# Twelve operand tiles laid out first in SBUF, each beginning at a multiple of 2048 bytes

## The chip, the cores and the metric

The kernel runs on one core of a Trainium2 chip. The metric is the device time of one launch in microseconds (us). [...]

## The reference

Linear attention over 8 batches of 8 heads, 576 positions and 64 channels per head; its 4608 x 512 result runs through two feed-forward networks with a squared ReLU.

```python
q_s = softmax of q over channels;  k_s = softmax of k over positions
kv = einsum('bhsd,bhse->bhde', k_s, v);  attn = einsum('bhsd,bhde->bhse', q_s, kv)
x = attn.transpose(0, 2, 1, 3).reshape(4608, 512)
x = relu(x @ w_in)**2 @ w_out          # 512 -> 2048 -> 512
x = relu(x @ w2_in)**2 @ w2_out        # 512 -> 2048 -> 512
```

## The kernel before

Tokens go in nine blocks (j) of 512, the hidden width in 16 chunks (f) of 128, or 8 pairs (a), or 4 units (u). Every fp32 operand of a large product is split into a high and a low part, and `passes` (line 400) issues three matmuls for a term: low x high, high x low, high x high. A matmul on PE is two instructions: LDWEIGHTS loads the stationary operand (128 columns), MATMUL streams the moving one (256 or 512 columns) through it. PE goes through four stages:

- **h** (`h_mm`, 1728 matmuls of 512 columns): attention, block by block, and the first product of network 1, x against `w0`. Small matmuls of the attention (`kvps`, `xps`) lie between.
- **y0** (`second_mm`, l=0, 3024 matmuls of 256 columns): the second product of network 1. The moving operand is G (the hidden values), the stationary one W. A profile row calls it `y<-G,W`.
- **m** (`first_mm`, 3024 of 256): the first product of network 2, moving x, stationary W (`m<-x,W`).
- **y1** (`second_mm`, l=1, 3024 of 256): the second product of network 2. Here W moves and G is stationary (`y<-W,G`).

The last three use a seven-product scheme for 2 x 2 blocks (`LEFT`, `RIGHT`, `ORDER`, lines 36 to 38): `comb_add`, `comb_hi` and `comb_lo` (lines 76 to 97) make seven combinations, each with a high and a low part, of every operand. One call of `second` for one a is 7 results x 2 halves x 3 passes = 42 matmuls; a block j has 8 of them, 336 matmuls.

Operands live in twelve slots of 14,336 bytes per partition, `w0` to `w7` and `hl0` to `hl3`. A combination in a slot is 1024 bytes, a high part lies 7168 bytes from its low one, and a stationary operand is 512 bytes, so a moving operand begins at a multiple of 1024 bytes from its slot's start and a stationary one at a multiple of 512. W of pair a lies in `w{(a+5)%8}` (`slot_of`, line 706); G of block j, pair a in `hl{(8j+a+1)%3}`, but for the last four of a network (line 923); x of network 2 in two of the four `hl`. In stage h, chunk f of `w0` lies in slot `w{f//3}`, f = 15 in `hl3`, and x in `hl0` for an even j, `hl1` for an odd one, its last quarter in `hl3`. There too moving operands begin at multiples of 2048 and stationary ones at multiples of 512 from the slot's start.

`schedule` (line 542) sets the order of all instructions from planned costs and due times, once, when the kernel is built. It knows tags of slots, and no addresses. The tile pool gives each tag its place in SBUF when a tile of that tag is first asked for, one behind the other. This gives the slots these first bytes:

| slot | first byte | mod 512 | slot | first byte | mod 512 |
|---|---|---|---|---|---|
| w0 | 116416 | 192 | w6 | 52448 | 224 |
| w1 | 155392 | 256 | w7 | 66784 | 224 |
| w2 | 175936 | 320 | hl0 | 100032 | 192 |
| w3 | 9344 | 128 | hl1 | 190272 | 320 |
| w4 | 23680 | 128 | hl2 | 213824 | 320 |
| w5 | 38112 | 224 | hl3 | 136896 | 192 |

Of the kernel before, what the change touches and what calls it, by code (L numbers as in the profile page):

```python
# [8 lines left out]
F32 = mybir.dt.float32  # L9
# [11 lines left out]
P = 128  # L21
NP = H // 2
TB = 512
HB = TB // 2
# [17 lines left out]
def linear_attention_two_relu2_ffn(ctx: ExitStack, tc: tile.TileContext, q0, k0, eye, qh, kh, vh, wio, out):  # L42
# [10 lines left out]
    pool = ctx.enter_context(tc.tile_pool(name="sb", bufs=1))  # L53
    psum = ctx.enter_context(tc.tile_pool(name="ps", bufs=1, space=bass.MemoryType.PSUM))
    dram = ctx.enter_context(tc.tile_pool(name="dr", bufs=1, space=bass.MemoryType.DRAM))

    def f32(ap):
        return ap.bitcast(F32)
# [994 lines left out]
```

## Time and profile before

| | |
|---|---|
| median of 3 runs | 1610.34 us (1607.62 to 1617.39) |
| the profiled execution's own time | 1607.12 us |
| its span, first to last instruction | 1605.0 us |
| PE, busy | 1556.1 us (97%), 11,664 matmuls |
| PEld (LDWEIGHTS), busy | 1457.0 us (91%) |
| DVE, ACT, POOL busy | 74%, 59%, 25% |
| granted PE clock, mean | 0.991 |

Busy time of PE counts a matmul from its start to the modelled end of its pipeline, so that matmuls overlap in it: the mean duration of one says little, and the distance between the starts of two neighbours says what it costs. Where PE never stops, that distance is the length of a stretch divided by the matmuls that begin in it. Matmuls that still run at a stretch's edge are counted in it too.

### The profile page before, as it was taken

The page shows a single profiled execution, that of the slowest core. Times are in us where ns is not written, and L with a number is a line of the kernel's source. Part 1 is how long each engine was busy: PE and PEld are TensorE (multiplying, and loading weights), DVE is VectorE, ACT ScalarE, POOL GpSimd, SP SyncE. Part 2 cuts the span into 40 slices and gives each one's busy share as a digit, 9 for nine tenths or more (in the row PEclk, how much of TensorE's full clock was granted, in tenths as well). Part 3 has the DMA queues.
Part 4 walks back from the last instruction along what each step waited for, and adds up shares of the span by engine and source line. Part 5 has one row for each costly group of instructions (what it writes and reads, how often), then busy time and mean ns, then how long its engine had stood idle before and what let it go on. Part 6 is the DMA issues. An engine that isn't in the chain of part 4 may idle for free. (4 is left out here: it accounts for less than half of the span.)

```text
span 1605.0 us, 29964 instructions
## 1 busy us (share of the span) xinstructions
PE 1556.1 (97%) x11664; PEld 1457.0 (91%) x11664; DVE 1194.9 (74%) x1755; ACT 953.1 (59%) x1605; POOL 400.8 (25%) x332
## 2 busy tenths in 40 slices
PE   6799999999999999999998999999999899999998
PEld 4578888878888999999998999999999899999997
DVE  7998887777544988888889954553347898898885
ACT  7766766566554655555556877776667444333332
POOL 1000000000023333332323433333221443333322
PEclk9999999999999999999999999999999999999999
DMA  8547776676664443444434576663346344344332
GB/s 327 168 129 230 249 227 226 217 233 217 210 195 159 145 132 132 133 134 134 135 107 154 171 220 213 213 216 135 135 135 191 111 149 132 131 143 134 132 106 79
DMA packets 139135, 270.49 MB, mean 169 GB/s; under 512 B 12145, under 2 KB 71665, under 8 KB 138993
## 3 DMA queue, kind: packets, MB, share of 16 engines
q1 hardware_dynamic: 138992, 268.58, 51.2%
q8 instruction: 91, 1.49, 0.4%
q14 instruction: 52, 0.42, 0.1%
HBM read 161.58 MB, written 106.95 MB: 167 GB/s over the span
## 5 line engine op out<-in xcount | busy, mean ns | idle before, releaser
L404 PE MATMUL h<-hl,w 128*128 128x512 f32 x1620 | 395.7, 399 | 10.6 <-DVE w L64 10.6
L404 PEld LDWEIGHTS h<-hl,w 128*128 128x128 f32 x1620 | 303.7, 190 | 80.2 <-DVE w L64 10.0
L404 PE MATMUL m<-x,W 128*128 128x256 f32 x3024 | 362.2, 282 | 8.2 <-DVE W L97 5.3
L404 PEld LDWEIGHTS m<-x,W 128*128 128x128 f32 x3024 | 359.9, 189 | 9.8 <-DVE W L97 5.9
L404 PE MATMUL y<-W,G 128*128 128x256 f32 x3024 | 357.7, 280 | 7.8 <-DVE G L97 7.7
L404 PEld LDWEIGHTS y<-W,G 128*128 128x128 f32 x3024 | 356.3, 189 | 8.6 <-DVE G L97 8.4
L404 PEld LDWEIGHTS y<-G,W 128*128 128x128 f32 x3024 | 358.3, 189 | 0.7 <-DVE G L97 0.5
L404 PE MATMUL y<-G,W 128*128 128x256 f32 x3024 | 358.7, 281 | 0.3 <-DVE G L97 0.3
L92 ACT ACTIVATE G<-hl 128x512 fp32r<-128x512 f32 (+1 forms) x108 | 94.5, 889 | 163.7 <-PE y L404 101.7
L97 DVE TENSOR_TENSOR G<-hl,G 128x512 fp32r<-128x512 f32 (+1 forms) x108 | 121.5, 1126 | 34.3 <-ACT G L92 34.3
L434 POOL TENSOR_TENSOR ts<-ts,ts 128x512 f32<-128x512 f32 x54 | 85.0, 1574 | 245.2 <-ACT ts L431 218.7
L391 ACT ACTIVATE r<-h 128x512 f32<-128x512 f32 x144 | 84.9, 591 | 65.4 <-PE h L404 54.7
L443 DVE TENSOR_TENSOR t<-m,ts 128x512 f32<-128x512 f32 x72 | 49.7, 691 | 94.8 <-PE m L404 89.3
L258 POOL PARTITION_ALL_REDUCE m<-m x28 | 24.4, 872 | 337.5 <-DVE m L254 112.7
L449 ACT ACTIVATE t<-t 128x512 f32<-128x512 f32 x144 | 90.1, 629 | 2.8
L97 DVE TENSOR_TENSOR G<-att,G 128x1280 fp32r<-128x1280 f32 x50 | 75.8, 1516 | 10.4 <-ACT G L92 10.4
L97 DVE TENSOR_TENSOR G<-cf,G 128x1280 fp32r<-128x1280 f32 x50 | 77.3, 1546 | 8.4 <-ACT G L92 8.0
L92 ACT ACTIVATE G<-qd 128x512 fp32r<-128x512 f32 x40 | 25.3, 632 | 87.2 <-PE y L404 45.8
L92 ACT ACTIVATE G<-att 128x1280 fp32r<-128x1280 f32 x50 | 63.1, 1263 | 13.3 <-DVE att L84 13.3
L92 ACT ACTIVATE G<-cf 128x1280 fp32r<-128x1280 f32 x50 | 63.2, 1264 | 12.0 <-DVE cf L84 11.0
L446 ACT ACTIVATE t<-t 128x512 f32<-128x512 f32 x72 | 45.3, 629 | 38.9 <-DVE t L443 37.6
L92 ACT ACTIVATE G<-qc 128x512 fp32r<-128x512 f32 x40 | 25.3, 631 | 67.0 <-PE y L404 45.0
(162 smaller groups left out, 1991.0 us busy)
## 6 DMA issues: line engine op xcount, KB each, us to landing
g<-r SPq DMA_DIRECT2D x144, 256.0 KB, 3.5
g<-t SPq DMA_DIRECT2D x144, 256.0 KB, 2.8
hl<-g SPq DMA_DIRECT2D x64, 512.0 KB, 3.8
raw<-wio SPq DMA_DIRECT2D x48, 512.0 KB, 4.8
qc<-g SPq DMA_DIRECT2D x40, 512.0 KB, 3.8
qd<-g SPq DMA_DIRECT2D x40, 512.0 KB, 3.8
y<-t SPq DMA_DIRECT2D x72, 256.0 KB, 2.3
w<-wf SPq DMA_DIRECT2D x48, 256.0 KB, 4.8
```

Of the source, the lines that this page charges most:

```text
L92: nc.scalar.activation(out=hls[key][:, 0, r], in_=src, func=AF.Copy)
L97: nc.vector.tensor_tensor(out=hl[:, 1, r], in0=src, in1=f32(hl[:, 0, r]), op=ALU.subtract)
L258: nc.gpsimd.partition_all_reduce(m[:, 1, :P], m[:, 0, :P], P, bass.bass_isa.ReduceOp.max)
L391: nc.scalar.activation(out=r0[j, f].rearrange("p a b -> p (a b)"), in_=m.pop(("h", j, f)), func=AF.Relu)
L404: nc.tensor.matmul(ps, a, b, start=start, stop=True, skip_group_check=True)
L434: nc.gpsimd.tensor_tensor(out=t[k, "s5"], in0=t[k, "s5"], in1=t[k, "s2"], op=ALU.add)
L443: nc.vector.tensor_tensor(out=temp(k, q), in0=m[k, i], in1=t[k, "s5"], op=ALU.add)
L446: nc.scalar.activation(out=t[k, q], in_=t[k, q], func=AF.Relu)
L449: nc.scalar.activation(out=t[k, q], in_=t[k, q], func=AF.Square)
```

## The change

Right after the pools are opened, one tile of 896 bytes per partition and then one tile for each of the twelve slots are asked for. None of them is written or read. As a tag gets its place when it is first asked for, the twelve slots come first: from byte 2048 on (1152 bytes are taken by the DMA scratch and constants), 14,336 = 7 x 2048 bytes each, in the order w0 to w7, hl0 to hl3, and all others come behind them. Each slot's first byte is 0 mod 2048. The other tiles move too: the attention's operands (`kvbd`, `qd`) to multiples of 1024, the temporaries, sources and raw weights to other multiples of 32.

```diff
     dram = ctx.enter_context(tc.tile_pool(name="dr", bufs=1, space=bass.MemoryType.DRAM))
+
+
+    pool.tile([P, 224], F32, name="margin", tag="margin")
+    for tag in [f"w{i}" for i in range(8)] + [f"hl{i}" for i in range(4)]:
+        pool.tile([P, 14 * HB], F32, name=f"{tag}_room", tag=tag)
 
     def f32(ap):
```

All instructions of the five engines, their order, their waits and their shapes stay as they are; the addresses of their operands are all that differs.

## Rows read from the trace of the kernel before

**Rows 1.** Page, part 1: busy us (share of the span) xinstructions.
```profile
PE 1556.1 (97%) x11664; PEld 1457.0 (91%) x11664; DVE 1194.9 (74%) x1755; ACT 953.1 (59%) x1605; POOL 400.8 (25%) x332
```

**Rows 2.** Busy time by stage: stretch, length, busy (count) by engine, clock, DMA, GB/s.
```profile
100.00:504.53 404.53, 404.36 (x2178) 327.30 (x2177) 282.18 (x616) 249.23 (x584) 38.12 (x41) 1.00 0.66 214
504.53:863.38 358.85, 358.54 (x3025) 358.20 (x3024) 306.06 (x338) 208.69 (x236) 109.45 (x93) 1.00 0.41 134
863.38:1215.64 352.26, 344.11 (x2883) 342.48 (x2881) 191.77 (x244) 259.85 (x423) 117.80 (x82) 1.00 0.56 179
1215.64:1605.00 389.36, 373.74 (x3170) 372.75 (x3168) 327.08 (x360) 160.58 (x192) 123.81 (x98) 0.99 0.40 130
```

**Rows 3.** Page, part 5: PE's large groups, count, busy, mean ns, idle before.
```profile
L404 PE MATMUL h<-hl,w 128*128 128x512 f32 x1620 | 395.7, 399 | 10.6 <-DVE w L64 10.6
...
L404 PE MATMUL m<-x,W 128*128 128x256 f32 x3024 | 362.2, 282 | 8.2 <-DVE W L97 5.3
...
L404 PE MATMUL y<-W,G 128*128 128x256 f32 x3024 | 357.7, 280 | 7.8 <-DVE G L97 7.7
...
L404 PE MATMUL y<-G,W 128*128 128x256 f32 x3024 | 358.7, 281 | 0.3 <-DVE G L97 0.3
```

**Rows 4.** PE in whole blocks: y0, j 1-7; m, 2-7; y1, 2-7; h, 8.
```profile
545.02:823.41 278.39, 278.39 (x2355) 1.00 0.40 129
953.15:1191.52 238.37, 238.37 (x2018) 1.00 0.55 176
1321.50:1557.54 236.04, 236.04 (x2019) 1.00 0.39 130
460.36:504.53 44.17, 44.17 (x193) 1.00 0.51 169
```

**Rows 5.** PE in stage y0, block j=2, pairs a=3 to 7, one row each.
```profile
599.81:604.79 4.98, 4.98 (x44) 1.00 0.53 178
604.79:609.56 4.77, 4.77 (x44) 1.00 0.35 120
609.56:614.59 5.03, 5.03 (x45) 1.00 0.32 104
614.59:619.54 4.95, 4.95 (x45) 1.00 0.34 108
619.54:624.49 4.95, 4.95 (x45) 1.00 0.32 105
```

**Rows 6.** PE, one pair each: y0 j=4 a=3, j=5 a=4; y1 j=1 a=5, j=4 a=4.
```profile
679.36:684.39 5.03, 5.03 (x44) 1.00 0.34 116
...
724.11:728.87 4.76, 4.76 (x44) 1.00 0.33 110
...
1306.94:1311.96 5.02, 5.02 (x44) 1.00 0.23 79
...
1420.13:1424.90 4.77, 4.77 (x44) 1.00 0.60 204
```

**Rows 7.** PE in stage h: j=8 f=0-2, j=8 f=3-5, j=7 f=1-2, j=7 f=10-11.
```profile
460.36:468.53 8.17, 8.17 (x38) 1.00 0.67 221
468.53:476.93 8.40, 8.40 (x38) 1.00 0.48 149
...
416.69:422.26 5.57, 5.57 (x25) 1.00 0.83 244
442.98:448.54 5.56, 5.56 (x26) 1.00 0.67 229
```

**Rows 8.** Waits of PE: total us, times, longest us; the two longest.
```profile
PE h L404 <- DVE w L64: 10.6, 8, 2.7
PE y L404 <- DVE G L97: 8.0, 3, 6.9
```

**Rows 9.** VectorE at line 97, two sources: ns minimum/median/maximum, first and last start.
```profile
L97 DVE TENSOR_TENSOR G<-att,G x50: 1475/1485/2210, 462.0 to 1589.2; 128x1280 fp32r<-128x1280 f32 x50
L97 DVE TENSOR_TENSOR G<-cf,G x50: 1474/1486/2201, 464.2 to 1584.2; 128x1280 fp32r<-128x1280 f32 x50
```

## The prediction

> **What bounds the kernel now.** I began with the page's first part: PE is busy for 97% of the span, no other engine for more than 74% [rows 1]. The busy time by stage then shows where it ever stops. Through the 404.53 us of stage h that follow the first 100 it is busy for 404.36, through the 358.85 of y0 for 358.54 [rows 2]; the large groups had to wait 10.6, 8.2, 7.8 and 0.3 us in all, beside 1474 us of busy time [rows 3], and the longest sums of waits are for VectorE's operands at a stage's start [rows 8]. So the time is PE's own pace: the distance between the starts of two neighbouring matmuls, times their number. PEld, which loads the next matmul's stationary operand, is busy for 358.20 of y0's 358.85 us [rows 2]: two streams out of SBUF run side by side all the time, the moving operand and the next stationary one.
>
> The next thing to see is that this pace is not one number. [...] Within one block of y0 five neighbouring pairs of 42 matmuls take 4.98, 4.77, 5.03, 4.95 and 4.95 us [rows 5]. The length of a pair repeats for the same two slots in other blocks [rows 5, 6].
>
> What orders these lengths is where the two operands lie. I call **offset** the first byte of the moving operand's slot less that of the stationary one's, mod 512; inside a slot both operands begin at multiples of 512, so every matmul of a pair has the same one. With G's and W's slots from the table of places, the five pairs have the offsets 128 (hl2, w0), 448 (hl0, w1), 0 (hl1, w2), 192 (hl2, w3) and 64 (hl0, w4). The two slowest numbers of the table recur at offset 0: 5.03 us again for hl0 over w0, and 5.02 in y1, where w2 moves over hl2. The quickest recur at 448: 4.76 for hl0 over w1, 4.77 in y1 for w1 over hl1 [rows 6]. Offset 0 is thus seen with slots at 192 and at 320 mod 512, and with either operand in either role; 448 with a moving slot at 192 and at 256. Shifting both operands together changed nothing, shifting one against the other changed 5%. The slots that this compares lie at many distances, so the rest of the address seems to matter little.
>
> For 512 columns the order is another one. In stage h 36 matmuls at offset 0 take 8.17 us, 226.9 ns each, and 36 at offset 448 take 8.40, 233.3 ns; offsets 128 and 192 (block 7: 24 matmuls in 5.57 and in 5.56) cost 232.1 and 231.7 [rows 7]. There offset 0 is the best.
>
> **The change part by part.** No instruction is added, removed or moved on any queue; the extra tiles are neither written nor read. What changes is that all twelve slots begin at 0 mod 512, so **every large matmul gets offset 0**.
>
> The 256-column stages: I price one matmul at 5.03 / 42 = 119.8 ns, the rows of offset 0. y0: 3024 x (119.8 - 118.4) = +4.4 us. m: 3024 x (119.8 - 118.2) = +4.7. y1, the quickest now: 3024 x (119.8 - 117.1) = +8.2. Together +17.3 us, all on the path, as PE's starts are the path. The least certain is m, whose operands change slots every six matmuls, so that no stretch of it shows an offset by itself; without it the sum would be +12.6.
>
> Stage h: even blocks cost 230.1 ns [rows 4], odd ones 232.1 and 231.7 where rows show them [rows 7], 230.9 over five even and four odd. Offset 0 gives 226.9, 4.0 less. Block 0 lies in the first 100 us, where PE waits 10.6 us for operands [rows 8] and would only wait longer; 8 x 192 = 1536 matmuls are left, 6.1 us at most. Small matmuls of the attention cut into seven of these eight blocks, and the row of 226.9 is from the undisturbed one, so I take three quarters: -4.6 us. This gain needs suppliers that keep up with a PE under 2% quicker: in that stage VectorE is busy for 282 of 404.53 us, ScalarE for 249, DMA for 0.66 of its time [rows 2], so they do.
>
> Not priced: the attention's own matmuls, some 640 of the 2178 in stage h. Their places change too and no row separates them; at the 6.2 ns between the ends of [rows 5] they are 4.0 us either way, and I take nothing. VectorE, ScalarE and POOL write and read at new places; the same VectorE instruction has medians of 1485 and 1486 ns from its two sources `att` and `cf`, which lie apart and write to all `hl` slots [rows 9], so I take nothing there either, and if some got longer, PE's slower pace in m, y0 and y1 gives them room.
>
> Sum: +17.3 - 4.6 = **+12.7 us**. Against the profiled execution's own 1607.12 us (span 1605.0) that is 1619.8; against the median of the runs shown, 3.2 us above that execution, 1623.0. I forecast 1622. The forecast's own range is 1615 (m gains nothing) to 1628 (nothing comes back in h).
>
> **The rivals.**
>
> *Places do not matter* (0.10). The lengths of the pairs would then come from what else runs beside them, such as VectorE's and POOL's accesses, and stay. Time 1607 to 1610. Against it: the same length returns for the same slots in other blocks and in y1, beside other work [rows 5, 6]. [...]
>
> *Straddling, and so faster* (0.15). All slow pairs at offset 0 have both operands at an odd multiple of 64 bytes, where a read might cross lines that an even place does not; the quick ones have one at an even multiple (w1 at 256). No row has both at an even one, which is what the change makes. If that were the cause, all 256-column matmuls would go at 4.77 / 42 = 113.6 ns: 3024 x (4.8 + 4.6 + 3.5) = -39.0, with -4.6 in h -43.6 us: about 1565. Against it: in stage h both operands at an odd multiple is the best case, not the worst [rows 7]; and a pair with w3 at 128 or w4 at 128, even multiples as well, took 4.95, not 4.77 [rows 5].
>
> *Slower by more, no gift in h* (0.13). Offset 0 was seen in h only with x in hl0 and w0. If two streams at the same multiple of 2048 disturb each other at 512 columns as they do at 256, stage h goes to the worst it shows, 233.3 ns instead of 230.9: 1536 x 2.4 = +3.7 in place of -4.6. Then +21.0: 1628 by the profiled execution, 1631 by the median, over 1% slower. The point from which it decides: a block of 192 matmuls over 44.4 us.
>
> That the change does not do what it says is ruled out by the places themselves: the twelve first bytes are 2048 + 14336 i.
>
> **How the numbers follow.** The forecast has 0.62. About 1% (16 us) is what a measurement of this kernel can tell from no change; my +12.7 lies just inside it, and with what h may fail to give back and some us between medians about a quarter of it, 0.16, lies outside. Slower by over 1%: 0.16 + 0.13 = 0.29. Within 1%: 0.46 + 0.10 = 0.56. Faster by over 1%: 0.15. The range goes from 1606 (nothing changes) to 1633 (the third rival on the median, with 2 us for the runs' scatter) and leaves out the second rival and a tail.
>
> **What would show it.** In the changed kernel's profile a block of 336 matmuls in y0, m and y1 should take 40.2 us each, where now it is 39.8, 39.7 and 39.3; a pair 5.03 us everywhere, with no 4.77 left; stage h's last block 43.6 us for 44.17; VectorE's medians at 1485 ns. PE's waits in the large groups should stay near 27 us. Pairs that keep their old mixture speak for the first rival, pairs at 4.77 for the second. The forecast is wrong as well if offset 0 with both slots at an even place has a length of its own that no row shows.

## The result, and the profile after

The changed kernel takes **1623.58 us** in the median (1617.73 to 1628.77, 7 runs) where the kernel before, run beside it, takes 1610.69 (1607.62 to 1617.39, 7 runs): a ratio of 1.0069, 95% interval [1.0048, 1.0091]. It is slower by 0.7%, clear of noise and within 1%. The forecast was 1622, its range 1606 to 1633. The profiled execution has a span of 1620.1 us (before 1605.0) and a time of its own of 1622.16 (before 1607.12).

The busy time of each stage, with the columns of [rows 2], for stage h after its first 100 us, y0, m and y1:

```profile
100.00:504.19 404.19, 400.82 (x2180) 327.18 (x2179) 282.63 (x617) 249.19 (x585) 38.72 (x41) 1.00 0.66 215
504.19:867.06 362.87, 362.87 (x3026) 362.87 (x3024) 305.98 (x339) 209.09 (x236) 110.23 (x93) 1.00 0.39 132
867.06:1222.53 355.47, 348.91 (x2882) 347.49 (x2881) 190.96 (x243) 259.63 (x423) 117.34 (x82) 1.00 0.54 178
1222.53:1620.10 397.57, 382.77 (x3170) 382.11 (x3168) 327.55 (x360) 160.32 (x192) 118.78 (x98) 0.99 0.37 127
```

Against [rows 2] the stages are longer by -0.34, +4.02, +3.21 and +8.21 us, 15.1 in all, which is the whole difference of the two spans. In the last three it is PE's busy time that grew, by 4.33, 4.80 and 9.03 us; the time in which PE stood still there shrank from 24.1 to 21.4 (6.56 in m and 14.80 in y1). In stage h it is the other way: PE is busy for 3.5 us less and stands still for 3.37 us where it was 0.17.

Whole blocks, as in [rows 4] (length of the stretch, PE's busy time and count, granted clock as a share of full speed, DMA):

```profile
544.50:826.74 282.24, 282.24 (x2355) 1.00 0.38 128
955.61:1198.05 242.44, 242.22 (x2018) 1.00 0.53 174
1329.84:1571.76 241.92, 241.92 (x2019) 1.00 0.37 127
460.67:504.19 43.52, 43.52 (x194) 1.00 0.52 174
```

The three 256-column stages now run at one pace: 282.24 / 2352 = 120.0 ns, 242.44 / 2016 = 120.3 (with 0.22 us of stops in it), 241.92 / 2016 = 120.0. In block j=2 of y0 pairs a=3 and 4, and in stage h the first 36 matmuls of the last block:

```profile
599.94:604.98 5.04, 5.04 (x45) 1.00 0.54 176
604.98:610.02 5.04, 5.04 (x45) 1.00 0.30 107
460.67:468.83 8.16, 8.16 (x38) 1.00 0.61 194
```

The mixture of [rows 5] is gone: pair a=3 took 4.98, a=4 took 4.77, and both take 5.04 now. Stage h's 36 matmuls take 8.16 us, as only w0's did [rows 7], and its whole last block goes at 43.52 / 192 = 226.7 ns, whatever the slot. VectorE's two instructions at [rows 9] keep their medians to 1 ns:

```profile
L102 DVE TENSOR_TENSOR G<-att,G x50: 1473/1486/2198, 463.2 to 1604.1; 128x1280 fp32r<-128x1280 f32 x50
L102 DVE TENSOR_TENSOR G<-cf,G x50: 1474/1485/2204, 465.4 to 1599.6; 128x1280 fp32r<-128x1280 f32 x50
```

And this is what PE waited for in stage h from 100 us on (total us, times, longest):

```profile
PE xps L372 <- DVE qhl L69: 2.1, 3, 1.4
PE h L409 <- ACT hl L66: 0.7, 1, 0.7
PE h L409 <- DVE hl L69: 0.6, 2, 0.4
```

That is 3.4 us. The kernel before has one wait in that stretch, 0.2 us for `qhl`.

### The profile page after: what moved, and what is told of

It is laid out like the page before. It is cut to its first block, busy times and chain, and to the rows that moved or that the text cites. A ratio compares the mean times of both kernels' runs of the same rounds, so it can differ in the third digit from the quotient of the medians.

```text
span 1620.1 us, 29964 instructions
## 1 busy us (share of the span) xinstructions
PE 1570.7 (97%) x11664; PEld 1475.9 (91%) x11664; DVE 1194.9 (74%) x1755; ACT 953.1 (59%) x1605; POOL 396.7 (24%) x332
## 5 line engine op out<-in xcount | busy, mean ns | idle before, releaser
L409 PE MATMUL m<-x,W 128*128 128x256 f32 x3024 | 367.3, 284 | 6.6 <-DVE W L102 5.4
L409 PE MATMUL y<-W,G 128*128 128x256 f32 x3024 | 366.5, 284 | 6.9 <-DVE G L102 6.9
L409 PEld LDWEIGHTS m<-x,W 128*128 128x128 f32 x3024 | 365.3, 193 | 8.0 <-DVE W L102 6.0
L409 PEld LDWEIGHTS y<-W,G 128*128 128x128 f32 x3024 | 365.4, 193 | 7.4 <-DVE G L102 7.3
L409 PEld LDWEIGHTS y<-G,W 128*128 128x128 f32 x3024 | 363.0, 192 | 0.1
L409 PE MATMUL y<-G,W 128*128 128x256 f32 x3024 | 363.0, 283 | 0.0
```

The costliest lines, as they stand in the source:

```text
L409: nc.tensor.matmul(ps, a, b, start=start, stop=True, skip_group_check=True)
```

## The experiments

All are edits of the changed kernel, and in all of them the instructions and their order stay the same. "Offset" is, as in the prediction, the first byte of the moving operand's slot less that of the stationary one's, mod 512. The experiments ran in three groups, each beside the kernel before; its median there was 1615.59, 1612.86 and 1611.31 us, so times are compared within a group and by ratios. Each trace is of one execution, and the start of a launch varies: the 2178th matmul before the first of y0 begins between 99.7 and 104.6 us in the eleven kernels' traces, at a granted clock of 0.88 to 0.93 over the first 100 us. Where the length of stage h matters, it is therefore given from this matmul on too.

The theory: the offset sets PE's pace. The rival: each operand's own place sets it, and what is slow is an even place.

### Everything 64 bytes further: all64

```diff
-    pool.tile([P, 224], F32, name="margin", tag="margin")
+    pool.tile([P, 112], F32, name="margin", tag="margin")
```

> All twelve slots begin at 64 mod 512 (and not at multiples of 2048), so the offset between moving and stationary operand stays 0. Theory (the offset between the two operands sets PE's pace): as the changed kernel, 120 ns for every 256-column matmul, 40.3 us per block of 336, span 1620 within 3 us. Rival (each operand's own place sets it, an even place is the slow one): both operands leave it, pace back to 118 or below, span 1605 or less.

Measured: ratio 1.008 [1.0063, 1.0096], as slow as the changed kernel. Whole blocks of y0, m and y1:

```profile
549.67:831.90 282.23, 282.23 (x2354) 1.00 0.38 128
960.45:1202.57 242.12, 242.12 (x2018) 1.00 0.55 174
1334.40:1576.32 241.92, 241.92 (x2018) 1.00 0.38 127
```

The lengths are those of the changed kernel to 0.32 us, with every slot at an odd multiple of 64 bytes and no longer at one of 2048. The rival that even places are slow falls. The span, 1624.6, lies a little over the 1623 that was expected: 4.5 us over the changed kernel's, of which 3.6 arise before the 2178th matmul, where the first 100 us have a granted clock of 0.90 here and of 0.93 there.

### One operand 64 bytes from the other: w64 and hl64

```diff
-    pool.tile([P, 224], F32, name="margin", tag="margin")
-    for tag in [f"w{i}" for i in range(8)] + [f"hl{i}" for i in range(4)]:
+    pool.tile([P, 96], F32, name="margin", tag="margin")
+    for tag in [f"hl{i}" for i in range(4)]:             # hl64: the eight w first
+        pool.tile([P, 14 * HB], F32, name=f"{tag}_room", tag=tag)
+    pool.tile([P, 16], F32, name="pad", tag="pad")
+    for tag in [f"w{i}" for i in range(8)]:              # hl64: the four hl behind them
         pool.tile([P, 14 * HB], F32, name=f"{tag}_room", tag=tag)
```

> hl slots at 0 mod 512, w slots at 64: offset 448 in y0, m and h, 64 in y1. Theory: y0 and m go at 113.4 ns (38.1 us per block of 336), y1 at 113.4 or 117.8 ns (38.1 to 39.6 us), stage h at 233.3 ns (last block of 192: 44.8 us). Against the changed kernel -40 us in y0 and m, -7 to -20 in y1, +8 in h: span 1568 to 1582. Rival (each operand's own place): one of two operands leaves the even place, so less than all64 gains: span between 1605 and 1620.

> w slots at 0 mod 512, hl slots at 64: offset 64 in y0, m and h, 448 in y1. Theory: y1 at 113.4 ns (38.1 us per block of 336), y0 and m at 113.4 or 117.8 ns (38.1 to 39.6 us), h at 229 ns (last block of 192: 44.0 us): -20 us in y1, -13 to -40 in y0 and m, +2 in h, span 1560 to 1588. Rival (each operand's own place): as w64, between 1605 and 1620.

Measured: w64 ratio 0.9901 [0.9881, 0.9921], profiled span 1594.3; hl64 ratio 0.9876 [0.9832, 0.992], profiled span 1599.8, and one of its four runs at 1586.95 us where the others lie at 1599.56 to 1601.88. Whole blocks of y0, m and y1 and stage h's last block, w64:

```profile
547.22:813.78 266.56, 266.56 (x2355) 1.00 0.41 136
942.47:1179.90 237.43, 237.43 (x2018) 1.00 0.55 177
1309.23:1546.67 237.44, 237.44 (x2018) 1.00 0.39 129
462.80:507.55 44.75, 44.75 (x194) 1.00 0.50 168
```

and hl64:

```profile
552.77:829.79 277.02, 277.02 (x2355) 1.00 0.40 130
959.81:1197.25 237.44, 237.44 (x2018) 1.00 0.56 177
1325.15:1553.63 228.48, 228.48 (x2018) 1.00 0.40 134
```

Sixty-four bytes between the two kinds of slot are worth some 2% of the kernel against all64 (0.9901 and 0.9876 over 1.008). Where the offset is 448 (y0 of w64, y1 of hl64) a matmul costs 266.56 / 2352 = 228.48 / 2016 = 113.3 ns; where it is 64 (y1 of w64, y0 of hl64) 237.44 / 2016 = 277.02 / 2352 = 117.8. Swapping which slots were shifted swapped the quick stage from y0 to y1, as the operands' roles swap there. The rival, by which both spans would lie between 1605 and 1620, falls. But the theory as it stood missed both spans too (1568 to 1582 and 1560 to 1588). In w64 the miss is m, which has offset 448 and runs at 237.43 / 2016 = 117.8 ns, not 113.4: at an offset of 448 the run shows two paces. In hl64 most of it is stage h, which ends 8.8 us later than in the changed kernel where 2 was expected; 3.8 of them arise before the 2178th matmul.

### All offsets in one run: sweep64 and sweep32

```diff
-    pool.tile([P, 224], F32, name="margin", tag="margin")
-    for tag in [f"w{i}" for i in range(8)] + [f"hl{i}" for i in range(4)]:
+    pool.tile([P, 96], F32, name="margin", tag="margin")
+    for tag in [f"hl{i}" for i in range(4)]:
         pool.tile([P, 14 * HB], F32, name=f"{tag}_room", tag=tag)
+    for i in range(8):
+        if i:
+            pool.tile([P, 16], F32, name=f"pad{i}", tag=f"pad{i}")    # sweep32: 8
+        pool.tile([P, 14 * HB], F32, name=f"w{i}_room", tag=f"w{i}")
```

> hl slots at 0 mod 512, slot w0 at 0, w1 at 64, and so on to w7 at 448: one run shows eight offsets in y0 (0, 448, 384, ... 64 for w0 to w7) and the eight negative ones in y1 and, for w0 to w4, in h. Theory: in y0 a pair of 42 takes 5.04 us with W in w0 and 4.77 with W in w1; 4.95 to 4.99 at offsets 64, 128, 192 and 384, as the kernel before showed; 256 is open: 5.0 if only the parity of 64 bytes counts. Rival (each operand's own place): pairs differ by w's place alone, so the order over w0 to w7 is the same in y0 and in y1; the theory has it reversed, w7 quickest in y1.

> hl slots at 0 mod 512, slot w0 at 0, w1 at 32, and so on to w7 at 224: offsets 0, -32, ... -224 in y0 and 0, 32, ... 224 in y1. Theory with a period of 256: pairs in w0 5.04 us, w2 4.77, w4 4.98 and w6 4.95 in y0, as the sweep by 64 had them at offsets 0, 448, 384 and 320; the odd multiples of 32 lie between 4.90 and 5.05, as the kernel before showed for w5 to w7. Rival (each operand's own place): the same order over the slots in y0 and y1.

One block of y0 in sweep64, pairs a=0 to 7 with W in w5, w6, w7, w0, w1, w2, w3, w4, which makes the offsets 192, 128, 64, 0, 448, 384, 320, 256:

```profile
632.08:636.87 4.79, 4.79 (x44) 1.00 0.63 221
636.87:641.83 4.96, 4.96 (x44) 1.00 0.33 111
641.83:646.78 4.95, 4.95 (x44) 1.00 0.38 126
646.78:651.83 5.05, 5.05 (x45) 1.00 0.53 184
651.83:656.59 4.76, 4.76 (x44) 1.00 0.36 117
656.59:661.57 4.98, 4.98 (x44) 1.00 0.33 106
661.57:666.52 4.95, 4.95 (x44) 1.00 0.31 106
666.52:671.57 5.05, 5.05 (x45) 1.00 0.31 107
```

The second four repeat the first four to 0.03 us: in this run the pattern has a period of 256 bytes. Among these offsets PE is slowest at 0 and 256 (5.05), then 128 and 384 (4.96 to 4.98), 64 and 320 (4.95), and quickest at 192 and 448 (4.76 to 4.79). In y1 the sign is reversed; pairs with W in w7, w1 and w3, offsets 448, 64 and 192:

```profile
1414.16:1418.95 4.79, 4.79 (x44) 1.00 0.49 164
1423.97:1428.92 4.95, 4.95 (x44) 1.00 0.58 200
1433.91:1438.69 4.78, 4.78 (x44) 1.00 0.31 110
```

w1 is quick in y0 and not in y1, w7 and w3 the other way round; a slot's own place cannot do that. sweep32 shows the odd multiples of 32; its y0 pairs with W in w7, w0, w1, w2 and w3, offsets 288, 0, 480, 448 and 416:

```profile
639.36:644.31 4.95, 4.95 (x44) 1.00 0.42 132
644.31:649.34 5.03, 5.03 (x44) 1.00 0.52 171
649.34:654.30 4.96, 4.96 (x44) 1.00 0.39 121
654.30:659.07 4.77, 4.77 (x45) 1.00 0.33 109
659.07:664.11 5.04, 5.04 (x44) 1.00 0.32 105
```

Half a step away from 448 the quick pace is gone, on both sides (4.96 us at 480, 5.04 at 416, for 4.77); at 416 PE is as slow as at 0 (5.03).

### The quick offset everywhere: best

hl slots at 128 mod 256, w slots 64 bytes further mod 256, and G of network 2 written 128 bytes into its slot, so that y1 has the same offset as y0 and m, 192 mod 256.

```diff
-    pool.tile([P, 224], F32, name="margin", tag="margin")
-    for tag in [f"w{i}" for i in range(8)] + [f"hl{i}" for i in range(4)]:
+    for tag in [f"hl{i}" for i in range(4)]:
+        pool.tile([P, 14 * HB + 64 * (tag != "hl3")], F32, name=f"{tag}_room", tag=tag)
+    pool.tile([P, 16], F32, name="pad", tag="pad")
+    for tag in [f"w{i}" for i in range(8)]:
         pool.tile([P, 14 * HB], F32, name=f"{tag}_room", tag=tag)
...
-            hls[key] = pool.tile([P, 2, 7, HB], F32R, name=key, tag=tag)
+            lo = 32 if key.startswith("G1") else 0
+            hls[key] = pool.tile([P, 14 * HB + lo], F32R, name=key, tag=tag)[:, lo:].rearrange("p (s c n) -> p s c n", s=2, c=7)
```

> hl slots at 128 mod 256, w slots at 192 mod 256, and G of network 2 written 128 bytes into its hl slot: offset 192 mod 256 in y0, m and y1 (and in h, where no gain or loss is expected, since PE there waits for the attention when it is quick). Theory (offset mod 256 sets the pace; at 64 off the parity of the even ones two paces are possible, 113.3 and 117.8 ns, and a stop of PE chooses): 113.3 ns in y0 and y1 (38.1 us per block of 336), m at 113.3 or 117.8 ns; against the kernel before -14 us in y0, -11 in y1, -1 to -14 in m: ratio 0.975 to 0.984. Rival (only the places mod 512 seen so far are quick, the period is not 256): half the pairs at 117.8, ratio 0.985 or more.

Measured: 1587.72 us in the median (1584.8 to 1591.33, 5 runs) where the kernel before takes 1612.86: ratio **0.9839 [0.9819, 0.9859]**, 1.6% faster than before and at the edge of what was expected. Whole blocks of y0, m and y1:

```profile
555.88:822.44 266.56, 266.56 (x2354) 1.00 0.42 136
949.28:1185.03 235.75, 234.65 (x2018) 1.00 0.55 178
1314.57:1543.05 228.48, 228.48 (x2018) 1.00 0.41 134
```

y0 and y1 both hold 113.3 ns, in every pair, so the rival with half the pairs at 117.8 falls. Stage m does not, and two stretches of 20 us show it change its pace:

```profile
1025.00:1045.00 20.00, 20.00 (x179) 1.00 0.76 232
1056.00:1076.00 20.00, 20.00 (x172) 1.00 0.70 220
```

Seven matmuls more begin in the first. Between the two, two starts come late, 266 ns (at 1046.8 us) and 781 ns (at 1054.1) behind the one before them, and the distance between starts is 113.3 ns before the first of these stops and 117.8 behind it and to the end of the stage.

The gain is less than the three stages give. Against the kernel before, the profiled executions are shorter by 13.6 us in y0, 4.9 in m and 9.2 in y1, 27.7 in all, and stage h ends 11.9 us later: 4.9 of that arises before the 2178th matmul, and from there on the stage takes 411.8 us where the kernel before takes 404.8. No loss was expected there. Its last block goes at 44.75 / 192 = 233.1 ns where offset 0 gave 226.7: the distance that is quickest for 256 columns (113.3 ns) is a slow one for 512.

### Bringing m into the quick pace: kick

best, with W of pair 3 in the first product of network 2 written 192 bytes into its slot (`48 if key == "W2_3"` in the line above, and 256 bytes more for slot w0).

> As best, and W of pair 3 in the first product of network 2 lies 192 bytes into its slot, so that its 378 matmuls have offset 0. Theory (a stretch at offset 0 brings the following ones at offset 192 mod 256 into the quick pace, as it did in the sweep for slot w1 behind w0): m runs at 113.4 ns but for this pair's 120, 38.4 us per block of 336, whatever pace it began with; the pair itself costs 378 x 6.7 ns = 2.5 us; ratio 0.973 to 0.978, with less scatter than best. Rival (the pace is set at a stop alone and then kept): m stays at 117.8 ns where best has it, and the kernel is 1 us slower than best.

Measured: 1591.98 us (1586.84 to 1606.22, 6 runs), ratio 0.9888 [0.9854, 0.9921]; no gain over best and more scatter. The length of six blocks of m:

```profile
946.66:1184.54 237.88, 237.88 (x2019) 1.00 0.55 177
```

237.88 / 2016 = 118.0 ns, so the idea failed; the rival, a pace set at stops alone, does not fit either, as the next rows show. They are 84 matmuls before the first at offset 0, a stretch across that one, and 126 matmuls after it:

```profile
903.88:913.39 9.51, 9.51 (x86) 1.00 0.65 218
914.10:918.10 4.00, 4.00 (x35) 1.00 0.60 211
928.61:943.45 14.84, 14.84 (x128) 1.00 0.78 231
```

The first take 9.51 / 84 = 113.2 ns each, the last 14.84 / 126 = 117.8. PE stopped at 913.6 and then not before 943.7. In between, the starts lie 113.3 ns apart up to 916.15 us, where the first matmuls with the shifted operand run, five of them 120 ns apart; from there to the next stop no two starts are nearer than 117 ns. So here matmuls at offset 0 took the quick pace away without a stop. What selects the pace in general is not settled.

### Stage h by itself: h448

The changed kernel, run again (after2), and with `w0`'s chunks 64 bytes into their slots, which makes the offset of stage h 448 and leaves the rest alone.

```diff
-... w_hi(f, lambda: part2(room, lo)), [y], [place, wf[0]])
+... w_hi(f, lambda: part2(room, lo + (0 if f == NF - 1 else 16))), [y], [place, wf[0]])
```

> The changed kernel once more, as the base for h448 on the same chip: 120 ns per 256-column matmul, h at offset 0 (226.9 ns).

> The changed kernel with w0's chunks 64 bytes further into their slots: offset 448 in stage h for 15 of its 16 chunks, 0 elsewhere as before. If PE's pace sets stage h (the prediction's step), each matmul costs 233.3 in place of 226.9 ns: 8 blocks x 180 x 6.4 = +9.2 us, less the 3 us that PE waits in the changed kernel: +6 us or more. If the preparation of the attention's operands sets it (as the prediction's miss suggests), PE's waits there vanish and the stage ends within 2 us of after2.

Measured: 1623.87 us (1623.35 to 1628.93, 4 runs; ratio 1.0084 [1.0064, 1.0105]) and 1630.04 (1628.99 to 1632.46, 4 runs; ratio 1.0119 [1.0099, 1.0139]), 6.2 us apart. Stage h from 100 us on, after2:

```profile
100.00:505.13 405.13, 402.27 (x2184) 1.00 0.67 215
```

and h448:

```profile
100.00:511.76 411.76, 410.78 (x2193) 1.00 0.66 211
```

So the pace of stage h does count. The medians differ by the +6 us that the first of the two expectations named; in the traces 2.6 of the 6.6 us arise before the 2178th matmul, and from there on the stage takes 404.2 and 408.3 us, 4.1 more. That is over the 2 us of the second expectation, and that the attention's preparation alone sets the stage falls. PE's stops shrink from 2.86 to 0.98 us as it slows. What holds here is between the two: the slower PE lengthened the stage by 4.1 us, and part of what the quicker one gained went into waits. One wait in after2 came with a fall of the clock: behind the 2.25 us that PE waited for `qhl`, the 2.99 us from 237.70 on have a granted clock of 0.50, and matmuls of 512 columns start 427 ns apart there, for the 226.7 of the changed kernel's last block at a clock of 1.00.

## Why the prediction was right, step by step

*PE's pace is the time, and the offset sets it*: right. The three stages' added busy time is 4.33 + 4.80 + 9.03 = 18.2 us where the sum had 4.4, 4.7 and 8.2, 17.3. Its paces of before come from [rows 4]: 278.39 / 2352 = 118.4 ns in y0, 238.37 / 2016 = 118.2 in m, 236.04 / 2016 = 117.1 in y1 (unrounded, the rows make 4.2, 4.6 and 8.1, 16.9). The rows of offset 0 were 5.02 and 5.03 us for a pair, the pace that stays is 5.04: the pairs of before that [rows 5] and [rows 6] show at offset 0 began with some shorter distances, 112 ns in the first, 118, 116 and 118 in the second, 113 to 121 over the first eight in the third, and went on at 120. That the pace depends on no operand's own place was read from a handful of rows; all64 and the sweep show it. Stage m, the least certain term, came out as priced in busy time. "All on the path" was too much: the stages grew by 15.4 us, as 1.6 us of stops went out of m and 1.1 out of y0 and y1. In m it is the waits for ScalarE that shrank, from 2.6 to 1.0 us.

*Stage h gives 4.6 us back*: the step that failed. The matmuls went at 226.7 ns, as priced (36 in 8.16 us; the rows of "128 and 192" that it was priced against are mixed, as a quarter of x lies in hl3, at offsets 0 and 64), and PE's busy time fell by 3.5 us, but the stage ended only 0.34 us earlier. The sentence at fault is that suppliers "so they do" keep up, because VectorE was busy for 282 of 404.53 us. A mean share says nothing of a chain: `qhl`, which VectorE makes for the attention's small matmuls, comes late now, and the waits for it and for x took 3.4 us, 3.2 more than before. Behind the longest of them, 1.37 us, stands an engine that the prediction did not count among the suppliers. VectorE was idle itself until POOL's all-reduce of the maxima of k (`m`) was done. The kernel before, and the changed one, at the same place (lines between these are left out):

```profile
230.54 0.72 POOL L258 PARTITION_ALL_REDUCE m<-m  x1 [5.76 <-DMA w<-wf]
231.29 0.83 DVE L262 TENSOR_TENSOR att<-att,m 128x640 f32<-128x640 f32 x1 [1.74 <-POOL m L258]
```

```profile
226.79 0.29 DVE L259 TENSOR_TENSOR m<-m,att 128x128 f32<-128x128 f32 x1
232.46 0.72 POOL L263 PARTITION_ALL_REDUCE m<-m  x1 [8.00 <-issue]
233.21 0.83 DVE L267 TENSOR_TENSOR att<-att,m 128x640 f32<-128x640 f32 x1 [4.94 <-POOL m L263]
233.96 0.68 DVE L69 TENSOR_TENSOR qhl<-qT,qhl 128x512 fp32r<-128x512 f32 x1
234.69 0.39 PE L372 MATMUL xps<-qhl,kvbd 128*128 128x256 f32 x1 [1.37 <-DVE qhl L69]
```

The all-reduce began 5.4 us after VectorE had finished its input, where it took 2.2 before. In every run 27 of the 28 all-reduces begin within 0.3 us of theirs, and this one does not: it lags by 5.4 to 6.4 us in after, after2, all64, hl64, sweep64 and best, where PE's longest wait for `qhl` is 1.4 to 2.4 us, and by 1.4 to 3.6 in before, w64, h448, kick and sweep32, where it is at most 0.7. best is among the late ones with PE as slow in stage h as in w64 and kick, so a quicker PE is not the whole reason. What holds this all-reduce back stays open: the profile names a DMA in the kernel before, and nothing ("issue") in the changed one.

In the profiled execution the sum came to 15.0 us of the 12.7 forecast: stage h gave 4.3 us less than priced, and the three other stages cost 1.9 less. Two misses of opposite sign thus cancel in part. In the medians the difference is 12.9 us, which is nearer than the working deserves, and that is luck.

*Nothing else moves*: right for VectorE as far as rows show, as its medians stay. For the attention's own matmuls too: in the last 2178 matmuls before y0 the 457 distances between starts of `kvps` sum to 17.67 us before and 17.66 after, and those between `xps` matmuls grew by 2.2 us, of which 2.1 are the waits for `qhl`.

*The rivals.* "Places do not matter" is refuted by all64 and w64, which differ in places alone and by 28 us in their medians, 1628.44 and 1599.98: the pace of PE moves between 113.3 ns (w64, y0) and 120.0 (all64, y0) with the distance of two operands, at a granted clock of 1.00. "Straddling" falls with the change itself: both operands at an even place cost 120.0 ns, no less than both at an odd one (282.23 / 2352 = 120.0 in y0 of all64). "No gift in h" falls as a mechanism: 43.52 us for the last block, not 44.4. Its outcome, that stage h gives nothing back, came nearly true all the same, by waits.

What is shown is that the offset between moving and stationary slot decides, but for 192 mod 256, where two paces occur (113.3 and 117.8 ns). That it is the read of the next stationary operand, beside the streaming one, that disturbs it, is only argued: PEld works beside PE through all of y0 (362.87 of 362.87 us), which fits it, but a matmul's own stationary operand has the same offset as the next one's, and no run told them apart.

## What to carry to other kernels

Where PE never stops, divide stretches of the trace by their matmuls and group them by where the two operands lie: one shape at several paces, 113.3 to 120.0 ns, was a question of layout here, and a kernel that mixes all cases by accident is a free experiment on each. Giving every operand the same place mod 256, as aligning them all to a large power of two does, was among the worst layouts here for 256-column matmuls (120.0 ns); a distance of -64 bytes mod 256 between moving and stationary operand was the best (113.3 ns in y0 and y1 of best), and was worth up to 5.6% of a matmul. For 512 columns it was the other way round (226.7 ns at offset 0, 233.1 at 448), so price each shape from its own rows. Before taking credit for a quicker stage, look at who delivers its operands late next, and at who delivers to that engine, not at their mean share.

## What the runs showed of the hardware that was not expected

- The distance between matmuls of 256 fp32 columns went with the offset, with a period of 256 bytes over the eight offsets of sweep64: 120.0 ns at 0 (after), 117.8 at 64 (w64), 4.98 us / 42 = 118.6 at 128 (sweep64, at 384), 113.3 or 117.8 at 192 (w64, at 448).
- At 512 columns the order differed: 226.7 ns at offset 0 (after), 44.75 / 192 = 233.1 at 448 (w64).
- At offset 192 mod 256 two paces occurred, 113.3 and 117.8 ns. PE kept the first over 2352 matmuls in y0 of best, and left it in m at a stop of 266 ns there, in kick at a few matmuls with offset 0. One of four runs of hl64 was 13 us quicker than the rest and has no trace. The two paces do not explain it: in hl64 only y1 has that offset, and there the traced run, one of the other three, has the quick pace, 113.3 ns, already.
- One all-reduce of 28, always the same, begins 1.4 to 6.4 us after its input is ready, the other 27 within 0.3 us, in each of the eleven traces.
